# Masking the transposed probabilities instead of the right-hand side in the second pass of a decode-attention backward kernel

**Chip, cores, metric.** One core of one Trainium2 chip. The metric is the device time of one execution in microseconds (us), the median of several runs.

## The reference, cut to what matters

```python
# one token, D=448; 16 query heads on 8 key/value heads, Dh=256
# cache of Sk=32768 rows, of which the last W=4096 are attended
k = repeat(k_cache[:, :, Sk-W:, :], 2);  v = repeat(v_cache[:, :, Sk-W:, :], 2)
p = softmax(q @ k.T / 16);  o = p @ v
h = x + o.reshape(...) @ wo;  h2 = h + gated_mlp(layernorm(h))
# wanted: h2, and by vjp the gradients of x, k_cache, v_cache, wq, wo, and the three mlp weights
```

The gradients of the two caches have the shape of the caches: 8 x 32768 x 256 bf16 each, 134 MB. Only the last 4096 rows of each head are not zero. The kernel therefore writes 235 MB of zeros, and that is most of what it moves.

For one key/value head g the non-zero part is two sums of two outer products: dV = p0 x do0 + p1 x do1, and dK = ds0 x q0/16 + ds1 x q1/16, each over 4096 keys and 256 columns. The second pass computes them with 32-row products on TensorE.

## The kernel before

The engines go by their short names: PE is TensorE, DVE VectorE, ACT ScalarE, POOL GpSimd; SP is SyncE, which issues transfers, and SPq is its queue. An eviction is the copy of a product out of its PSUM tile (here 512 columns of `d_ps`, 684 ns on DVE and 589 on ACT in the kernel before). The zero transfers ("fills") are issued on the GpSimd queue from the start, 55 of them at first and 48 more in the middle of the kernel. What is left of them ("late jobs", 5 transfers, 18.9 MB) follows on the SP queue near the end:

```python
late_jobs = [(out_2, G - 1, 5, 7, 2 * ZW), (out_3, G - 1, 0, 6, 2 * ZW), (out_3, G - 1, 6, 7, ZW)]
...
send_fills(0, HALF0)
send_fills(HALF0, HALF1, True)
```

The second pass, for each head (cuts marked by ...):

```python
pds = work2.tile([128, 4, 8, 4], bf16, tag="pds")      # 4 q x 8 l tiles of keys; p0, p1, ds0, ds1
...
r_ps = ps_t.tile([128, 128], bf16, tag="tmp")
nc.tensor.transpose(r_ps[:], pds[:].rearrange("p q l i -> p (q l i)"), ident_bf[:])
rT = work2.tile([128, 128], bf16, tag="rT")
nc.vector.tensor_copy(out=rT[:], in_=r_ps[:])           # row 32q + 4l + i, column: key
nc.vector.tensor_copy(out=Zr, in_=...)                  # do0, do1, q0/16, q1/16, repeated 32 times
R_ps = ps_t.tile([128, 2, 2, 128], f32, tag="tmp")
... 4 products ...
R_sb = work2.tile([128, 512], bf16, tag="R", bufs=1)
nc.scalar.copy(out=R_sb[:], in_=R_ps[:]...)
RB_ = Rbig[it % 2]                                      # the mask: 8 copies of R, one for each l
nc.vector.tensor_tensor(out=RB_, in0=R_sb[:].unsqueeze(1).to_broadcast([128, 8, 512]),
                        in1=tl_f[:].unsqueeze(2).to_broadcast([128, 8, 512]), op=ALU.mult)
for l in range(8):
    for qp in range(2):
        d_ps = ps_d.tile([128, 2, 2, Dh], f32, tag="d")
        for qi in range(2):
            q = 2 * qp + qi
            nc.tensor.matmul(d_ps[:, qi]..., lhsT=rT[32*q:32*(q+1), :], rhs=RB_[32*q:32*(q+1), l, :], ...)
        # evictions: ScalarE for qp = 1, VectorE for qp = 0, into stV and stK
for o_ap, st_ in ((out_3, stV), (out_2, stK)):
    LD.dma_start(out=o_ap[0, g, Sk - W:, :]..., in_=st_)
```

A product reads 32 rows: the 4 rows of each of 8 key tiles l. `tl_f` is the 0/1 mask that leaves only the 4 rows of one l. It may be applied to either factor.

## Time and profile before

| | before |
|---|---|
| time | 798.8 us, later runs included 798.96 us (798.65 to 799.29) |
| bytes | 334.76 MB, 420 GB/s over the span |
| DVE busy | 437.1 us, 55% |
| PE busy | 478.9 us, 60% |
| ACT busy | 196.0 us, 25% |

The table is read with one caution: busy shares are averages over the span.

### The profile page before, as it was taken

The page shows a single profiled execution, that of the slowest core. Times are in us where ns is not written, and L with a number is a line of the kernel's source. Part 1 is how long each engine was busy: PE and PEld are TensorE (multiplying, and loading weights), DVE is VectorE, ACT ScalarE, POOL GpSimd, SP SyncE. Part 2 cuts the span into 40 slices and gives each one's busy share as a digit, 9 for nine tenths or more (in the row PEclk, how much of TensorE's full clock was granted, in tenths as well). Part 3 has the DMA queues.
Part 4 walks back from the last instruction along what each step waited for, and adds up shares of the span by engine and source line. Part 5 has one row for each costly group of instructions (what it writes and reads, how often), then busy time and mean ns, then how long its engine had stood idle before and what let it go on. Part 6 is the DMA issues. An engine that isn't in the chain of part 4 may idle for free.

```text
span 797.2 us, 7318 instructions
## 1 busy us (share of the span) xinstructions
PE 478.9 (60%) x2926; PEld 222.6 (28%) x2926; DVE 437.1 (55%) x629; ACT 196.0 (25%) x309; POOL 61.8 (8%) x112
## 2 busy tenths in 40 slices
PE   0459999999999999251409478684450553722000
PEld 0334434344344333121208334331220211310000
DVE  2116584765846782263690679579653784964000
ACT  0142314134132201010102126353330442534000
POOL 4000000010101111100210001010000000000000
PEclk9989999999999999555558779766555556765555
DMA  9999999999999999999999999999999999999995
GB/s 349 431 430 430 428 431 430 430 428 430 430 423 427 427 419 413 423 421 424 432 428 423 424 431 431 428 425 427 424 424 422 424 424 424 423 427 418 433 434 247
DMA packets 29352, 334.76 MB, mean 420 GB/s; under 512 B 2819, under 2 KB 5894, under 8 KB 7814
## 3 DMA queue, kind: packets, MB, share of 16 engines
q0 software_dynamic: 16496, 216.01, 64.0%
q1 hardware_dynamic: 11382, 116.68, 34.8%
q10 hardware_dynamic: 1440, 1.61, 0.6%
q8 instruction: 23, 0.38, 0.2%
q14 instruction: 11, 0.09, 0.0%
HBM read 53.69 MB, written 280.59 MB: 419 GB/s over the span
## 4 chain that ended last, share of the span: by engine, by line
PE 37%; DMA 32%; DVE 16%; ACT 4%; issue 2%; another core or an unknown queue 0%; SPq 0%; DVEq 0%; ACTq 0%
DMA out_dram<-arena 19%; PE M_ps L317 12%; PE ok_ps L320 7%; PE rows_ps L256 6%; PE tr_ps L253 4%; DMA dh_bc<-in_grad_out_dram 4%; DMA arena<-in_A_k_cache_dram 4%; DMA arena<-in_B_w_down_dram 3%; ACT arena L270 2%; DVE arena L635 2%; DVE arena L459 2%; PE dqb_ps L502 2%; DMA arena<-in_B_w_gate_dram 2%; DVE arena L650 2%; PE d_ps L643 2%
## 5 line engine op out<-in xcount | busy, mean ns | idle before, releaser
L312 DVE TENSOR_TENSOR arena<-arena,p_f 128x2048 bf16<-128x2048 bf16 x64 | 145.4, 2286 | 61.6 <-PE M_ps L317 61.5
L317 PE MATMUL M_ps<-arena 128*128 128x512 bf16 x512 | 128.9, 380 | 0.2 <-ACT arena L323 0.2
L643 PE MATMUL d_ps<-arena,rT 32*128 32x512 bf16 x256 | 46.6, 529 | 111.0 <-DVE arena L651 63.9
L253 PE MATMUL tr_ps<-ident_bf,arena 128*128 128x128 bf16 x1024 | 92.5, 242 | 19.6 <-ACT arena L611 11.2
L256 PE MATMUL rows_ps<-arena,vpad 128*16 128x512 bf16 x256 | 90.6, 451 | 19.9 <-DVE arena L613 14.6
L133 POOL DMA_DIRECT2D out_dram<-arena x90 | 48.6, 542 | 538.5 <-DMA out_dram<-arena 491.3
L253 PEld LDWEIGHTS <-arena 128*128 128x128 bf16 x1024 | 69.0, 108 | 73.8 <-issue 64.4
L270 ACT COPY arena<-tr_ps 128x1024 bf16<-128x1024 bf16 x64 | 61.8, 1015 | 64.7 <-PE tr_ps L253 64.7
L647 ACT CAST arena<-d_ps 128x512 bf16<-128x512 f32 x64 | 37.7, 589 | 128.4 <-PE d_ps L643 128.3
L320 PE MATMUL ok_ps<-arena 128*16 128x512 bf16 x256 | 63.8, 381 | 0.9 <-DVE arena L297 0.9
L317 PEld LDWEIGHTS <-arena 128*128 128x128 bf16 x512 | 43.3, 99 | 59.0 <-issue 23.2
L611 ACT COPY arena<-tr_ps 128x1024 bf16<-128x1024 bf16 x32 | 32.6, 1019 | 94.6 <-PE tr_ps L253 36.4
L650 DVE CAST arena<-d_ps 128x512 bf16<-128x512 f32 x64 | 43.8, 684 | 16.9 <-PE d_ps L643 16.4
L651 DVE CAST arena<-d_ps 128x512 bf16<-128x512 f32 x64 | 43.5, 679 | 11.2 <-DMA out_dram<-arena 11.2
L643 PEld LDWEIGHTS <-rT 32*128 32x128 bf16 x256 | 11.2, 96 | 136.5 <-issue 90.0
L648 ACT CAST arena<-d_ps 128x512 bf16<-128x512 f32 x64 | 38.1, 595 | 11.9 <-DMA out_dram<-arena 11.9
L635 DVE TENSOR_TENSOR arena<-R_sb,tl_f 128x4096 bf16<-128x4096 bf16 x8 | 35.4, 4419 | 0.7 <-ACT R_sb L633 0.7
L256 PEld LDWEIGHTS <-vpad 128*16 128x16 bf16 x256 | 19.1, 92 | 58.4 <-issue 51.3
L320 PEld LDWEIGHTS <-arena 128*16 128x16 bf16 x256 | 19.1, 89 | 41.6 <-issue 20.5
L514 DVE CUSTOM_DVE_ANT_0 arena<-arena 128x4096 bf16<-128x4096 bf16 x3 | 13.1, 4423 | 23.9 <-ACT arena L507 23.9
L285 ACT ACTIVATE e_f<-cols_ps,nbias 128x32 f32<-128x32 f32 x16 | 4.5, 286 | 86.8 <-DVE nbias L281 86.8
L258 DVE COPY arena<-rows_ps 16x512 f32<-16x512 f32 x16 | 10.8, 676 | 26.6 <-PE rows_ps L256 26.6
(198 smaller groups left out, 387.9 us busy)
## 6 DMA issues: line engine op xcount, KB each, us to landing
out_dram<-arena POOLq DMA_DIRECT2D x103, 2048.0 KB, 51.7
out_dram<-arena SPq DMA_DIRECT2D x18, 2048.0 KB, 32.3
arena<-in_A_v_cache_dram SPq DMA_DIRECT2D x10, 2048.0 KB, 50.0
arena<-in_A_k_cache_dram SPq DMA_DIRECT2D x8, 2048.0 KB, 29.2
out_dram<-arena SPq DMA_DIRECT2D x4, 4096.0 KB, 43.8
arena<-in_A_wq_dram SPq DMA_DIRECT2D x2, 3072.0 KB, 20.6
arena<-in_A_wo_dram SPq DMA_DIRECT2D x2, 1792.0 KB, 14.5
out_dram<-arena SPq DMA_DIRECT2D x2, 1792.0 KB, 15.1
```

Of the source, the lines that this page charges most:

```text
L133: ZQ.dma_start(out=reg, in_=zeros)
L253: nc.tensor.transpose(tr_ps[:, dh, i, :], X_sb[:, 4 * q + i, dh * 128:(dh + 1) * 128], ident_bf[:])
L256: nc.tensor.matmul(rows_ps[:], lhsT=pad[:, dh, 16 * q:16 * q + 16], rhs=XT[:, dh].rearrange("p t k -> p (t k)"), start=(q == 0 and dh == 0 ...
L270: sT_ps = dots(kv_at(K_off[g]), KT_slot, vpad[g % 2], rows1, ps_c, "cols", lambda q, XT, ps: nc.scalar.copy(out=XT, in_=ps))
L312: nc.vector.tensor_tensor(out=pK, in0=K_sb[:, 4 * c:4 * c + 4, :].unsqueeze(2).to_broadcast([128, 4, 2, Dh]), in1=p_f[:, c::8, :].unsqueez ...
L317: nc.tensor.matmul(M_ps[:, vh, :], lhsT=V_sb[:, t, vh * 128:(vh + 1) * 128], rhs=pK[:, i, :, :].rearrange("p h d -> p (h d)"), start=(t == ...
L320: nc.tensor.matmul(ok_ps[:].rearrange("p k d -> p (k d)"), lhsT=ppad[g % 2][:, 8 * (t % 4) + t // 4, :], rhs=both(g, t), start=(g == 0 and ...
L635: nc.vector.tensor_tensor(out=RB_, in0=R_sb[:].unsqueeze(1).to_broadcast([128, 8, 512]), in1=tl_f[:].unsqueeze(2).to_broadcast([128, 8, 51 ...
L643: nc.tensor.matmul(d_ps[:, qi].rearrange("p w d -> p (w d)"), lhsT=rT[32 * q:32 * (q + 1), :], rhs=RB_[32 * q:32 * (q + 1), l, :], start=T ...
L648: nc.scalar.copy(out=stK[:, t:t + 2, :], in_=d_ps[:, :, 1, :])
L650: nc.vector.tensor_copy(out=stV[:, t:t + 2, :], in_=d_ps[:, :, 0, :])
L651: nc.vector.tensor_copy(out=stK[:, t:t + 2, :], in_=d_ps[:, :, 1, :])
```

## The change

Its intent: the mask goes on the small factor. The transposed probabilities have 128 columns, and 8 masked copies of them make 1024 columns a head; the right-hand side has 512, and 8 copies make 4096. The mask also takes over the copy of the transposed tile from PSUM.

```diff
-            rT = work2.tile([128, 128], bf16, tag="rT")
-            nc.vector.tensor_copy(out=rT[:], in_=r_ps[:])
+            rTm = rT_slot[it % 2]
+            nc.vector.tensor_tensor(out=rTm, in0=r_ps[:].unsqueeze(1).to_broadcast([128, 8, 128]),
+                                    in1=tl_f[:].unsqueeze(2).to_broadcast([128, 8, 128]), op=ALU.mult)
 ...
-            R_sb = work2.tile([128, 512], bf16, tag="R", bufs=1)
-            nc.scalar.copy(out=R_sb[:], in_=R_ps[:].rearrange("p w e n -> p (w e n)"))
-            RB_ = Rbig[it % 2]
-            nc.vector.tensor_tensor(out=RB_, in0=R_sb[:].unsqueeze(1).to_broadcast([128, 8, 512]),
-                                    in1=tl_f[:].unsqueeze(2).to_broadcast([128, 8, 512]), op=ALU.mult)
+            R_sb = R_slot[it % 2]
+            nc.scalar.copy(out=R_sb, in_=R_ps[:].rearrange("p w e n -> p (w e n)"))
 ...
-   lhsT=rT[32 * q:32 * (q + 1), :],     rhs=RB_[32 * q:32 * (q + 1), l, :]
+   lhsT=rTm[32 * q:32 * (q + 1), l, :], rhs=R_sb[32 * q:32 * (q + 1), :]
```

Cut: the two lines that place the new buffers where the large ones were.

More of the change, by code (lines that the diff above doesn't have):

```diff
@@ L87 @@
     rows2 = ar(RB + 47 * KB, 2 * KB)[0:16].bitcast(f32)
-    Rbig = [ar(RB + 8 * KB * i, 8 * KB).rearrange("p (l n) -> p l n", l=8) for i in range(2)]
+    rT_slot = [ar(RB + 2 * KB * i, 2 * KB).rearrange("p (l n) -> p l n", l=8) for i in range(2)]
+    R_slot = [ar(RB + (4 + i) * KB, KB) for i in range(2)]
     dK_off = [RB + 16 * KB, A_off[2]]
@@ L642 @@
                         q = 2 * qp + qi
-                        nc.tensor.matmul(d_ps[:, qi].rearrange("p w d -> p (w d)"), lhsT=rT[32 * q:32 * (q + 1), :], rhs=RB_[32 * q:32 * (q + 1), l, :],
+                        nc.tensor.matmul(d_ps[:, qi].rearrange("p w d -> p (w d)"), lhsT=rTm[32 * q:32 * (q + 1), l, :], rhs=R_sb[32 * q:32 * (q + 1), :],
                                          start=True, stop=True)
```

## The prediction

The sum came to 0 us: up to 8 x 3.4 = 27 us of compute, given back in waits for transfers. Two things in it stay as estimates: the cost of the new mask, from a line through two measured DVE durations, and the 2 us each way of (c), which the range rests on.

> **What bounds the kernel now.** I read the 40 slices of the page first, because the share of an engine over the whole span mixes stages, and then the DMA totals.
>
> ```profile
> PE   0459999999999999251409478684450553722000
> DVE  2116584765846782263690679579653784964000
> DMA  9999999999999999999999999999999999999995
> GB/s 349 431 430 430 428 431 430 430 428 430 430 423 427 427 419 413 423 421 424 432 428 423 424 431 431 428 425 427 424 424 422 424 424 424 423 427 418 433 434 247
> HBM read 53.69 MB, written 280.59 MB: 419 GB/s over the span
> ```
>
> The third row is what matters: the DMA engines are at 90% or more in every slice but the last, while PE and DVE swing between 0 and 9. The second pass, which the change touches, fills slices 24 to 37 (about 465 to 732 us), and there too the DMA row holds 9 and the rate holds 418 to 431 GB/s. The kernel moves 334 MB, most of it zeros for the untouched part of the caches, and does so at a nearly constant rate. The next question is whether the compute of the second pass decides anything at the end, so I read the busy time by stretches, the tail in particular.
>
> ```profile
> 460.00:500.00 40.00, 32.84 (x252) 16.46 (x252) 33.90 (x58) 18.89 (x28) 3.73 (x7) 0.84 1.01 431
> 540.00:580.00 40.00, 17.08 (x88) 6.54 (x88) 32.47 (x26) 11.76 (x21) 2.13 (x4) 0.59 1.01 425
> 580.00:620.00 40.00, 10.88 (x59) 4.31 (x58) 17.96 (x17) 5.74 (x9) 2.98 (x6) 0.54 1.01 425
> 740.00:760.00 20.00, 0.00 (x0) 0.00 (x0) 0.00 (x0) 0.00 (x0) 0.00 (x0) 0.50 1.01 430
> 760.00:780.00 20.00, 0.00 (x0) 0.00 (x0) 0.00 (x0) 0.00 (x0) 0.00 (x0) 0.50 1.02 437
> 785.00:790.00 5.00, 0.00 (x0) 0.00 (x0) 0.00 (x0) 0.00 (x0) 0.00 (x0) 0.50 0.67 288
> 790.00:797.20 7.20, 0.00 (x0) 0.00 (x0) 0.00 (x0) 0.00 (x0) 0.00 (x0) 0.50 0.08 34
> ```
>
> The columns are the stretch, its length, busy us of PE, PE weight loads, DVE, ACT and POOL, then clock, DMA share and GB/s. From 740 us to the end no compute engine does anything, and DMA still runs full until about 785. The timeline and the chain of waits say where this tail comes from:
>
> ```profile
> 717.75 11.95 SPq L663 DMA_DIRECT2D out_dram<-arena  x1
> 731.88 4.22 SPq L653 DMA_DIRECT2D out_dram<-arena  x2
> 738.32 5.52 SPq L663 DMA_DIRECT2D out_dram<-arena  x3
> ```
>
> ```profile
> 674.84 0.60 ACT arena L648
> 675.44 0.02 issue
> 675.46 42.29 DMA out_dram<-arena
> 717.75 0.02 issue
> 717.77 0.70 DVE arena L651
> ```
>
> The last head's gradients are handed to the queue at 731.88 us (2 transfers of 2.1 MB), followed by three late zero transfers (4.2, 4.2 and 2.1 MB): 14.7 MB. From 731.9 us to the end, the stretches move about 24.5 MB (8.1 us at 420, 20 at 430, 20 at 437, 5 at 410, 5 at 288, 7.2 at 34 GB/s). The difference, 9.8 MB, was already waiting in the queues when compute ended: some 23 us of DMA work at 430 GB/s. So compute ends with about 23 us to spare. The chain's last lines add that the last head was itself held: its evictions could start only at 717.77, when a transfer that had taken 42.29 us freed their buffer.
>
> [...] at 540 to 580 us DVE is busy for 32.47 of 40 us, at 580 to 620 for 17.96, and both move 425 GB/s. So less DVE work does not make transfers faster. [...] 4096 elements in 4419 ns is 0.93 elements a ns. [...]
>
> **The change part by part.**
>
> ```profile
> L635 DVE TENSOR_TENSOR arena<-R_sb,tl_f 128x4096 bf16<-128x4096 bf16 x8 | 35.4, 4419 | 0.7 <-ACT R_sb L633 0.7
> ```
>
> The same line on its own, who waited for it; and the two instructions beside it, which the change drops and keeps:
>
> ```profile
>   PE d_ps L643: 33.0, 5
>   PEld L643: 5.9, 1
> ...
> L626 DVE COPY rT<-r_ps x8: 205/214/216, 471.8 to 704.4; 128x128 bf16<-128x128 bf16 x8
> L633 ACT CAST R_sb<-R_ps x8: 586/603/604, 472.7 to 706.2; 128x512 bf16<-128x512 f32 x8
> ```
>
> The first two lines are the waits for the removed mask: PE and its weight loads, 38.9 us in 6 waits.
>
> Removed: 8 masks of 4.42 us (35.4 us) and 8 copies of 0.21 us (1.7 us), 37.1 us of DVE.
>
> Added: 8 masks of 1024 columns from PSUM. [...] 4096 elements in 4419 ns and, for the 64-element subtraction from PSUM, 213 ns give (4419 - 213) / 4032 = 1.043 ns an element and about 146 ns fixed. 1024 elements: 1068 + 146 = 1.21 us, in all 9.7 us. DVE falls by 27.4 us, from 437.1 to about 409.7.
>
> Moved: the masked operand of the product is now the stationary one. There are 256 weight loads of 128 columns for 256 products before (96 ns each), one for each product even where the weights repeat, and after as well; the moving side stays 512 columns. PE and ACT are unchanged in count and size. The mask now sits before the copy of R instead of after it: transpose, 1.21 us mask, R products, 0.6 us copy, instead of 0.21 us copy, R products, 0.6 us copy, 4.42 us mask. Both PSUM tiles share one buffer, so the R products must wait for the mask to finish reading: about 1.0 us more there. From transpose to first product a head gains 4.42 + 0.21 - 1.21 = 3.4 us, and evictions of the head before, which share DVE's order with the mask, are held 3.2 us less.
>
> On the path to the end: up to 8 x 3.4 = 27 us of compute chain, most of which the heads give back. From the third or fourth head on they wait for transfers to free the gradient buffers and the staging buffers (the chain has DMA pieces of 15.09, 29.29, 25.75, 22.43 and 42.29 us between 551 and 718 us). The last mask starts at 706.8 us and is over at 711.2, before the release at 717.77; so even the end of compute should hardly move, by 0 to a few us. If it came the full 27 us earlier, the bytes would still be the same 334.76 MB through a path that is already full: gains in the queue are only made of idle DMA time, and there is none between 36 us and 780 us. Sum: 0 us, plus or minus small reorderings.
>
> **The rivals.**
>
> (a) The second pass is compute-paced and shortens the whole by up to 27 us, to 772 us. For it: the SP queue's 90.6 us of waits for the DVE evictions in the second pass, and 38.9 us of waits for the mask itself. Against it: while SP waits, the zero fills of the other queue keep the engines full, so those waits leave no gap in the GB/s row. A last finish at 772 would need 334.76 MB at 434 GB/s over the whole span, start and drain included. I give it 1%.
>
> (b) A new wait takes the place of the old: the R products behind the longer read of the shared PSUM buffer, or a different order of instructions chosen when the kernel is built, which delays the last gradients. Compute could end 23 us later before DMA ran dry; a loss of 2% (16 us) would need compute about 39 us later, though the change shortens it. 1%.
>
> (c) The drain changes. The last 12 us run below full rate (288, then 34 GB/s) [...]. Which queue's packets are last can change with earlier heads: the SP queue gets more in earlier, the fill queue ends later. I allow 1 to 2 us each way, and as much for the rate: [...] a shift of 0.25% is 2 us.
>
> **Range and chances.** The middle is the time before, less nothing: 798.6 us. The three runs before spread 0.5 us; (c) adds about 2 us each way. Range 796.4 to 800.9. Chances: within 2% 0.98, faster 0.01, slower 0.01.
>
> **What would show it.** Right: DVE busy near 410 us; the new mask x8 at about 1.2 us; no product waiting for a 4.4 us mask; the DMA row still all nines at the same GB/s and 334.76 MB; compute over with DMA still running full for tens of us; longer waits for transfers in the later heads. Wrong: a gap in the DMA row before 780 us, a GB/s row that moved by over 1% in the second pass, or a last transfer issued later than about 755 us. The step I trust least is that the order of instructions stays close to that of before; the step that carries the result is that DMA has no idle time to give.

## The result, and the profile after

The changed kernel takes 798.96 us (798.87 to 799.10, 4 runs); the kernel before takes 798.96 us (4 runs). The ratio is 1.000, with a 95% interval from 0.998 to 1.002. Ratios here are the mean time of one kernel's fast runs over that of the other's of the same rounds, so not quite the ratio of the medians quoted.

The rows of the changed kernel by time slice:

```profile
DVE  2116584765846782263690678566925646644000
DMA  9999999999999999999999999999999999999995
GB/s 351 429 431 428 428 431 429 432 429 428 428 425 425 428 418 413 423 421 423 434 427 427 422 429 430 429 425 423 424 426 424 423 425 419 429 424 420 436 432 247
```

The DMA row is the same string as before, the GB/s row differs by at most 6 in any slice, and the bytes are again 334.76 MB. The DVE row is lighter in the second pass. The new mask, read as one line of the program (duration as min/median/max, then who waited for it):

```profile
L627 DVE TENSOR_TENSOR arena<-r_ps,tl_f x8: 1214/1218/1225, 472.2 to 701.0; 128x1024 bf16<-128x1024 bf16 x8
...
  PE R_ps L633: 1.3, 2
```

It costs 1218 ns, against 4420 before. DVE is busy for 410.6 us, 26.5 us less than before. The removed mask had held PE and its weight loads for 38.9 us; the new one holds the R products for 1.3 us in all. The change did on its engine just what it was meant to do, and the time did not move.

The SP queue at the end of the changed kernel, and two stretches of the tail (columns as in the prediction):

```profile
730.23 1.94 SPq L652 DMA_DIRECT2D out_dram<-arena  x2
732.65 14.76 SPq L662 DMA_DIRECT2D out_dram<-arena  x4
```

```profile
740.00:760.00 20.00, 0.00 (x0) 0.00 (x0) 0.00 (x0) 0.00 (x0) 0.00 (x0) 0.50 1.02 434
760.00:780.00 20.00, 0.00 (x0) 0.00 (x0) 0.00 (x0) 0.00 (x0) 0.00 (x0) 0.50 1.01 434
```

The last head's gradients are handed over at 730.23 us instead of 731.88. So compute ended only 1.65 us earlier although DVE had 26.5 us less to do. The waits in the second pass (460 to 740 us) show where the rest is. Each line is: who waited, for whom, us in total, times, longest. Before:

```profile
DVE arena L539 <- DMA out_dram<-arena: 22.0, 2, 15.4
...
DVE arena L651 <- DMA out_dram<-arena: 11.2, 2, 6.0
DVE arena L658 <- DMA out_dram<-arena: 10.6, 1, 10.6
...
DVE arena L551 <- DMA out_dram<-arena: 4.8, 1, 4.8
...
DVE arena L560 <- DMA out_dram<-arena: 3.8, 1, 3.8
```

After (the same lines of the program have moved by one):

```profile
DVE arena L540 <- DMA out_dram<-arena: 32.7, 3, 22.0
...
DVE arena L650 <- DMA out_dram<-arena: 17.0, 3, 9.9
...
DVE arena L657 <- DMA out_dram<-arena: 9.3, 1, 9.3
...
DVE arena L545 <- DMA out_dram<-arena: 7.0, 1, 7.0
DVE arena L561 <- DMA out_dram<-arena: 6.7, 1, 6.7
...
DVE arena L552 <- DMA out_dram<-arena: 4.9, 1, 4.9
```

Before, DVE waits 52.4 us in sum for transfers to free a buffer; after, 77.6 us. The difference, 25.2 us, and the 1.65 us of earlier end make 26.9 us, about the DVE time removed. DVE's other waits hardly changed: the largest, for the products of the second pass, was 16.4 us before and 15.2 after. So DVE is ready sooner and then waits longer for the buffer it writes to, which a transfer has yet to free. Only 5.8 of the 25.2 us are at the buffer of a head's gradients (L650, before L651); the rest is at buffers of the weight gradients' work (L540 to L561), less 1.3 us at the memset (L657).

### The profile page after: what moved, and what is told of

It is laid out like the page before. It is cut to its first block, busy times and chain, and to the rows that moved or that the text cites. A ratio compares the mean times of both kernels' runs of the same rounds, so it can differ in the third digit from the quotient of the medians.

```text
span 797.2 us, 7287 instructions
## 1 busy us (share of the span) xinstructions
PE 468.2 (59%) x2903; PEld 219.7 (28%) x2926; DVE 410.6 (51%) x621; ACT 196.0 (25%) x309; POOL 62.4 (8%) x112
## 2 busy tenths in 40 slices
DMA packets 29352, 334.76 MB, mean 420 GB/s; under 512 B 2819, under 2 KB 5894, under 8 KB 7814
## 4 chain that ended last, share of the span: by engine, by line
PE 40%; DMA 27%; DVE 15%; ACT 4%; issue 2%; another core or an unknown queue 2%; SPq 0%; DVEq 0%; ACTq 0%
DMA out_dram<-arena 18%; PE M_ps L318 13%; PE ok_ps L321 8%; PE rows_ps L257 7%; PE tr_ps L254 5%; DMA dh_bc<-in_grad_out_dram 4%; ACT arena L271 3%; DMA arena<-in_B_w_down_dram 3%; DVE arena L460 2%; PE dqb_ps L503 2%; DVE arena L649 2%; DMA arena<-in_B_w_gate_dram 2%; DVE arena L545 2%; DVE arena L650 2%
## 5 line engine op out<-in xcount | busy, mean ns | idle before, releaser
L313 DVE TENSOR_TENSOR arena<-arena,p_f 128x2048 bf16<-128x2048 bf16 x64 | 145.4, 2286 | 60.4 <-PE M_ps L318 60.4
L318 PE MATMUL M_ps<-arena 128*128 128x512 bf16 x489 | 125.3, 381 | 1.9 <-issue 1.0
L642 PE MATMUL d_ps<-arena 32*128 32x512 bf16 x256 | 45.1, 506 | 98.1 <-DVE arena L650 84.5
L257 PE MATMUL rows_ps<-arena,vpad 128*16 128x512 bf16 x256 | 87.6, 436 | 22.2 <-DVE arena L614 15.9
L254 PE MATMUL tr_ps<-ident_bf,arena 128*128 128x128 bf16 x1024 | 90.4, 238 | 16.6 <-DMA arena<-in_A_k_cache_dram 8.9
L254 PEld LDWEIGHTS <-arena 128*128 128x128 bf16 x1024 | 67.0, 106 | 69.0 <-issue 59.0
L646 ACT CAST arena<-d_ps 128x512 bf16<-128x512 f32 x64 | 37.7, 588 | 99.9 <-PE d_ps L642 99.9
L318 PEld LDWEIGHTS <-arena 128*128 128x128 bf16 x512 | 43.3, 99 | 59.0 <-issue 23.2
L650 DVE CAST arena<-d_ps 128x512 bf16<-128x512 f32 x64 | 43.6, 682 | 17.0 <-DMA out_dram<-arena 17.0
L649 DVE CAST arena<-d_ps 128x512 bf16<-128x512 f32 x64 | 43.9, 686 | 15.8 <-PE d_ps L642 15.2
L642 PEld LDWEIGHTS <-arena 32*128 32x128 bf16 x256 | 10.8, 95 | 123.6 <-issue 76.7
L647 ACT CAST arena<-d_ps 128x512 bf16<-128x512 f32 x64 | 38.2, 596 | 18.2 <-DMA out_dram<-arena 18.2
L540 DVE TENSOR_SCALAR arena<-arena,xT 128x1792 bf16<-128x1792 bf16 (+1 forms) x9 | 7.7, 883 | 32.7 <-DMA out_dram<-arena 32.7
## 6 DMA issues: line engine op xcount, KB each, us to landing
arena<-in_A_k_cache_dram SPq DMA_DIRECT2D x8, 2048.0 KB, 29.2
out_dram<-arena SPq DMA_DIRECT2D x2, 1792.0 KB, 15.2
```

Of the source, the lines that this page charges most:

```text
L254: nc.tensor.transpose(tr_ps[:, dh, i, :], X_sb[:, 4 * q + i, dh * 128:(dh + 1) * 128], ident_bf[:])
L257: nc.tensor.matmul(rows_ps[:], lhsT=pad[:, dh, 16 * q:16 * q + 16], rhs=XT[:, dh].rearrange("p t k -> p (t k)"), start=(q == 0 and dh == 0 ...
L313: nc.vector.tensor_tensor(out=pK, in0=K_sb[:, 4 * c:4 * c + 4, :].unsqueeze(2).to_broadcast([128, 4, 2, Dh]), in1=p_f[:, c::8, :].unsqueez ...
L318: nc.tensor.matmul(M_ps[:, vh, :], lhsT=V_sb[:, t, vh * 128:(vh + 1) * 128], rhs=pK[:, i, :, :].rearrange("p h d -> p (h d)"), start=(t == ...
L642: nc.tensor.matmul(d_ps[:, qi].rearrange("p w d -> p (w d)"), lhsT=rTm[32 * q:32 * (q + 1), l, :], rhs=R_sb[32 * q:32 * (q + 1), :], start ...
L646: nc.scalar.copy(out=stV[:, t:t + 2, :], in_=d_ps[:, :, 0, :])
```

## The experiments

The theory: the DMA engines are full from start to end, so only bytes count, and compute has slack. The rivals: (R1) the end of compute or the DVE work of the second pass sets the end, and some other delay happened to cancel the gain; (R2) the change never shortened the compute at all, for example because the shared PSUM buffer gave it back. Ten kernels ran, in three calls, each call on one chip with its own runs of the kernel before (medians 799.01, 798.99 and 798.85 us).

**The mirror of the change: the old mask done twice.**

```diff
+            for _ in range(2):
                 nc.vector.tensor_tensor(out=RB_, in0=R_sb[:]..., in1=tl_f[:]..., op=ALU.mult)
```

> The kernel before with its 4096-column mask done twice for each head (the second write repeats the first, the result stays right): the change's mirror, 8 x 4.42 = 35.4 us more DVE work. Theory (the DMA engines are full from start to end, compute has slack): DVE busy rises from 437 to about 472 us, the time stays at 799 us within 0.5%, the GB/s row stays at 418 to 434. Rival (the second pass is paced by DVE and the mask is on the path that sets the end): 20 to 35 us longer, 819 to 834 us.

Measured: 798.73 us, ratio to before 0.9995 (0.998 to 1.001), result correct. DVE is busy for 471.7 us, 34.6 us more than before. The end of its SP queue:

```profile
763.13 1.59 SPq L654 DMA_DIRECT2D out_dram<-arena  x2
764.77 2.52 SPq L664 DMA_DIRECT2D out_dram<-arena  x2
```

The last head is now handed over 31 us later than before, and still the time is the same; the DMA row is again all nines but for the last slice. The rival R1 expected 819 to 834 us. A change that adds 35 us of work to an engine costs as little here as one that takes 26.5 us away.

**How much slack: the last head alone held longer.** In the changed kernel the mask of the last head is written several times over.

```diff
+            for _ in range(19 if it == 7 else 1):      # 61 in the second run
                 nc.vector.tensor_tensor(out=rTm, in0=r_ps[:]..., in1=tl_f[:]..., op=ALU.mult)
```

> The changed kernel with the mask of the last head alone written 19 times instead of once: 18 x 1.22 = 21.9 us more, on the chain from the last head's transpose to its gradients. Theory: the last head is held by a transfer until 716 us anyway, and some 15 us of DMA work or more wait in the queues when compute ends, so compute ends at about 741 us instead of 730 and the time stays at 799 us (797 to 803). Rival (the end of compute sets the end): 821 us.

Measured: 799.16 us, ratio to before 0.9999 (0.9985 to 1.0014), correct. The last head went out at 742.55 us, as worked out, with two late zero transfers behind it where the changed kernel has four; R1 (821 us) falls.

```profile
742.55 1.63 SPq L653 DMA_DIRECT2D out_dram<-arena  x2
744.23 2.88 SPq L663 DMA_DIRECT2D out_dram<-arena  x2
```

> The same with 61 writes instead of one: 60 x 1.22 = 73 us more for the last head. Here the slack must be used up. Compute should end at about 792 us; the build puts all late zero transfers ahead of the last head's two in the SP queue, so only 4.2 MB are left then: 10 us at 430 GB/s and a drain of about 8 us. Theory: 806 to 815 us, with a gap in the DMA row before it. Rival (the end of compute sets the end, nothing is spare): 872 us. If the time stays under 803 us, the slack is larger than I worked out.

Measured: 810.97 us (808.44 to 812.34), ratio 1.015 (1.012 to 1.017), correct. The tail by stretches (PE, weight loads, DVE, ACT, POOL, clock, DMA share, GB/s), and its last issue:

```profile
760.00:780.00 20.00, 0.58 (x4) 0.41 (x4) 18.74 (x16) 0.07 (x1) 0.00 (x0) 0.50 0.93 400
780.00:785.00 5.00, 1.68 (x12) 0.32 (x11) 2.58 (x4) 2.66 (x5) 0.00 (x0) 0.50 0.18 75
785.00:790.00 5.00, 1.39 (x12) 0.22 (x8) 3.39 (x6) 2.92 (x6) 0.00 (x0) 0.50 0.01 3
```

```profile
795.92 0.93 SPq L653 DMA_DIRECT2D out_dram<-arena  x2
```

Here at last is the gap: DMA falls to 3 GB/s at 785 to 790 us and waits for the last head. The span of this profile is 808.3 us, so it is 12.4 us from that issue to its end. An estimate from this and from the span of 797.2 us of the kernel before: with all the late zeros ahead of it, the last head could go out at about 797.2 - 12.4 = 785 us before the time moved, some 53 us after the 731.88 us of the kernel before.

**Is there a gain that DMA hides? Both kernels without zero transfers.**

```diff
-    send_fills(0, HALF0)
-    send_fills(HALF0, HALF1, True)
...
-                send_fills(HALF1, len(fills))
...
-        for o, g, n0, n1, f in late_jobs: ...
```

The rows that should be zero are left unwritten, so the two cache gradients are wrong; the other seven outputs keep their small errors.

> The kernel before without any of the zero transfers (the untouched part of the two caches is not written, so the result is wrong on purpose if that memory isn't zero already). 99.9 MB are left, 232 us at 430 GB/s, so DMA can't bind the whole. Theory: the DMA row falls well below 9 in most slices and compute sets the time, about 530 to 600 us (an estimate: 797 us less the waits for slow transfers in both passes). What matters is the pair with a_no_fills.

> The changed kernel without the zero transfers. Theory (the change shortens the second pass's compute, and only the full DMA engines hide it): 15 to 27 us less than b_no_fills, 27 us being all of the DVE time removed. Rival (the removed mask was hidden beside other compute, or the later R products and the shared PSUM buffer give it back): less than 5 us.

Measured: 644.48 us (641.91 to 646.98) without the change, 621.37 us (621.07 to 621.90) with it: 23.0 us less by the means, a ratio of 0.964. R2 falls: the change does shorten the compute, nearly by the DVE time that it removes. The absolute guess of 530 to 600 us was too low by 44 us or more: the sum of waits that I had subtracted was too large, probably because waits of different engines overlap, which I did not check. The second pass from its start to shortly before its end, first without the change, then with it:

```profile
429.00:633.00 204.00, 125.06 (x878) 55.08 (x878) 183.23 (x239) 102.58 (x168) 0.00 (x0) 0.73 0.50 206
```

```profile
428.00:609.00 181.00, 119.02 (x878) 53.31 (x877) 156.77 (x231) 102.71 (x168) 0.00 (x0) 0.76 0.56 232
```

DMA moves 206 and 232 GB/s here, about half of the 420 GB/s that the kernel before moves over its span, and DVE is busy for 90% of the 204 us (183.23) and 87% of the 181 us (156.77). With the bytes gone, DVE is the main bound of this pass.

**Place or occupancy?** The 23 us could come from the DVE time or from the mask's new place ahead of the R products. So the new mask was written four times for each head, in the kernel without zero transfers.

> The changed kernel without zero transfers, with its mask of 1024 columns written four times for each head: 8 x 3 x 1.22 = 29.2 us of DVE work put back, about what the change took away (27.4), at the new place ahead of the R products. Theory (the 23 us between b_no_fills and a_no_fills are DVE occupancy in the second pass): 640 to 651 us. Rival (they come from where the mask stands, after the copy of R and in front of the products): 621 to 632 us.

Measured: 651.16 us (650.81 to 651.89), 0.2 us above what the theory expected and far from the rival's 621 to 632 us. That is 29.8 us above a_no_fills for 29.2 us of DVE work. (The two ran in different calls; the kernel before ran at 798.99 and 798.85 us in them.) So the new place is not free, and most of the 23 us are DVE occupancy. But the place counts too. The 29.2 us are a sum of durations; DVE's busy time rose by 27.1 us, from 409.1 to 436.2, which is almost that of b_no_fills (435.6 us), and yet this run is 6.7 us slower than b_no_fills. The four masks held the R products for 19.3 us in 6 waits, against 1.0 us in a_no_fills. The change itself gave 23.0 us for 26.5 us of busy time. The two stretches above show the other 3.5 us: DVE stood idle for 24.2 us with the change and for 20.8 without, and one of its evictions (L646, without the change L647) waited 15.6 us for products instead of 13.0. Why is not shown.

**Fewer bytes by degrees.**

```diff
+    del fills[-30:]       # and fills[-10:] in the second pair
```

> The kernel before without the last 30 of its 103 fills of 2.1 MB on the GpSimd queue: 62.9 MB less, 147 us at 427 GB/s (wrong on purpose as above). The fills then end at about 500 us, near the start of the second pass, and only the SP queue is left in it. Theory: the floor by bytes is 652 us; the queue runs dry in part of the second pass, so the time is 655 to 685 us with gaps in the DMA row after 500 us.

> The changed kernel without the same 30 fills. Theory: now that the SP queue is fed by compute alone, the change shows: 5 to 27 us less than b_30_fewer_fills, though not under the floor of 650 us. Rival (the change's compute gain isn't real or isn't on the path even here): within 3 us of it.

Measured: 711.99 us (709.90 to 714.83) and 700.84 us (700.49 to 701.12), a ratio of 0.984. My range for the first, 655 to 685 us, was too low: it took the bytes as the floor, while the second pass, once it is fed by one queue, runs at the pace of DVE (busy for 57.48 of the 60 us from 520 to 580). The change is worth 11 us here, half of 23. The end of the SP queue shows why, without the change first:

```profile
674.50 0.93 SPq L655 DMA_DIRECT2D out_dram<-arena  x2
675.48 3.78 SPq L665 DMA_DIRECT2D out_dram<-arena  x3
```

```profile
652.88 0.93 SPq L654 DMA_DIRECT2D out_dram<-arena  x2
653.86 5.10 SPq L664 DMA_DIRECT2D out_dram<-arena  x4
```

Compute ends 21.6 us earlier, but four late zero transfers stand behind the last head instead of three. One of them is 4.2 MB, 10 us at 425 GB/s, and 21.6 less 10 is the 11 us measured. The spans of the profiles agree: from the issue of the last head to the end it is 36.8 us without the change and 46.4 with it. So the order in which the build placed the late zeros took back half of the gain; this is read from the traces, and no run held the order fixed.

> The kernel before without the last 10 fills: 21.0 MB less, 49 us at 427 GB/s, so the floor by bytes is about 750 us. The fills end at about 685 us and the SP queue alone feeds the engines for the rest. Theory: 750 to 757 us, at most small gaps in the DMA row after 685 us.

> The changed kernel without the same 10 fills. Theory: 750 to 754 us, 0 to 5 us less than b_10_fewer_fills; if both sit at the floor the change is still worth nothing with 6% fewer bytes, and the loss of its gain is a matter of bytes against compute, not of this one placement of transfers.

Measured: 758.34 us (757.85 to 759.99) and 756.51 us (755.04 to 757.96), a ratio of 0.997. Both lie above the ranges expected, and 6.5 to 8 us above the floor that I worked out, because the queue does run dry in part after 640 us (slices at 259 to 362 GB/s in the first kernel, 306 to 351 in the second). The medians differ by 2 us, and the ranges overlap. In the profiled runs compute ends 9.6 us sooner with the change, again one more late transfer stands behind it, and the spans are 756.1 and 756.2 us. With 6% of the bytes gone the gain is still within noise.

No correct version beats both kernels. By this account a gain needs fewer bytes, or a DMA stream that starts and drains better; no run here tried the second.

## Why the prediction was right

- **The bound.** Right: DMA has no idle time to give. It moved 420 GB/s over the whole span, and 413 to 436 in slices 2 to 39 of the changed kernel; the DMA row was the same string, and 35 us of added DVE work, or 22 us on the last head, changed nothing.
- **The cost of the parts.** Right: 1.21 us predicted for the new mask, 1.218 measured; DVE 409.7 predicted, 410.6 measured (26.5 us less instead of 27.4: where DVE runs without a pause, an instruction starts some 0.08 us before the record of the last one ends, as at 473.34 us after a mask recorded from 472.21 to 473.42, so busy time is less than the sum of durations). The line of 1.043 ns an element and 146 ns fixed was an estimate that held for this mask; in the kernel before, it gives 2282 ns for the 2048-element TENSOR_TENSOR of L312, where 2286 was measured, but 1214 for the 1024-element bf16 copy of L613, where 682 was measured. PE's work did not grow: 256 products and 256 weight loads as before.
- **The heads give the gain back by waiting for transfers.** Right: DVE's waits for transfers grew by 25.2 us, and the end of compute moved by 1.65 us, "0 to a few". The prediction let these waits begin with the third or fourth head, at 551 us; the chain of the kernel before has one already at 492.82 us, of 15.66 us.
- **The slack.** Too small as a limit. The 23 us were worked out for the order of transfers that the kernel before has, and no run tested them in that order: in the runs whose last head was late, the build had moved late zeros ahead of it (two stood behind it in the +22 run and in the mirror, none in the +73 run), and with all of them ahead about 53 us are there. The prediction's warning sign, a last transfer issued later than about 755 us, was thus wrong: the mirror run issued at 767 us in the same time. So was its price for (b), 2% for compute 39 us later: the +73 run sent its last head 64 us later than the kernel before and lost 1.5%.
- **The shared PSUM buffer.** Right in direction, too large in size, and of no weight: about 1.0 us more was expected in each head, and the R products waited 1.3 us for the mask in all, in 2 waits.
- **The rivals.** (a), a second pass paced by compute, is a correct account of the kernel without its zero transfers and a wrong one of this kernel. (b), a reordering, did occur: the late zeros stood otherwise in the SP queue. It had no effect on the time while the engines were full, and by the traces cost 10 us where they were not. (c) did not show: the medians are equal, with an interval of about 1.4 us each way, and the drain looks alike (288 and 295 GB/s, then 34 and 33). In steps of 1 us the busy share of the 16 engines in the kernel before falls from full at 785 us to 0.27 at 789, and to 0.02 over the last 2.2 us. The 1.69 MB that it moves in the last 12.2 us would take 3.9 us at 430 GB/s, so the drain costs about 8 us, by this estimate. Why the share falls so, these runs do not show.

## What to carry to other kernels

Where the DMA row is full in every slice, as here, count bytes first. Work taken off another engine (26.5 us of DVE) turned into waits for transfers (25.2 us more), even though that engine was at 90% in some slices and the chain of waits ran through it. To see if a stage's compute matters, add work to it first: here a doubled cost that changed nothing (34.6 us more of DVE, ratio 0.9995) told, in one correct run, that the stage had slack. When the bytes go down later, measure such a change again, and look at which transfers stand behind the last computed ones. Putting those that depend on nothing ahead of them should help by this account, but no run here tried it as a change of its own.
